# A decode-attention kernel on one core: each tile of keys and values loaded in two transfers of 64 lanes, from two issuing engines

## The chip, the cores and the metric

The kernel runs on one core of one Trainium2 chip. Its engines are TensorE (PE), VectorE (DVE), ScalarE (ACT), GpSimd (POOL) and SyncE (SP); transfers between memory and the on-chip lanes are carried by the core's 16 DMA engines, on behalf of a queue that belongs to the engine that issued them. The metric is the device time of one execution in microseconds (us); lower is better.

## The reference, cut to what matters

Two branches share one layer-normed input and are summed with it. Branch A is attention with a cache: 4 sequences, one new token each, 32 heads of 128, 4096 cached positions. Branch B is a small gated MLP.

```python
q = (xn @ wq).reshape(4, 1, 32, 128).transpose(0, 2, 1, 3)
scores = einsum('bhqd,bhkd->bhqk', q, k_cache) * 128 ** -0.5
p = softmax(scores)
o = einsum('bhqk,bhkd->bhqd', p, v_cache)
A = o.transpose(...).reshape(4, 1, 4096) @ wo
B = gated_mlp(xn)                  # w_in 640 x 1728, w_out 864 x 640
return x + A + B
```

All inputs are bf16. k_cache and v_cache are 134.2 MB each; wq and wo are 5.2 MB each, w_in 2.2 MB, w_out 1.1 MB. Every byte is read once.

## The kernel before, in words

The work on the cache is cut into NT = 32 steps: a step i is one sequence b and one group hg of four heads (HT = 4, HG = 8 groups). Its keys are one tile of 128 lanes x 16384 bf16: the 4 x 4096 rows of 128 are laid over the lanes in order, so that a lane holds 128 consecutive rows (NC = 128), 32 KB in one piece in memory, and a tile has 4096 KB. Its values are a tile of the same form. Lanes 0 to 31 belong to the first head of the group, and so on.

Keys, values and the first weights live in a ring of five slots (pool `kv`, KV_SLOTS = 5; `slot`). `load(which, i)` (L118) takes a slot and issues the transfer; in the kernel before every such transfer is one instruction on SP (L123), except that of the last tile of values, which is cut along its rows into four (V_CUTS). `pump` (L140) issues loads in the fixed list `loads` (K0, K1, V0, K2, V1, K3, ...) as far as its bookkeeping `used` says that the occupant of the slot has been read. It is called once before the loop, once after the MLP, and at the end of every step.

A step (the loop at the end of the function) has the following parts. `product` (L457, DVE) multiplies a half of the key tile in place by the query; `fold_half` (L466, DVE) adds its two halves; `sums` (L475, PE) adds up the rest with the identity into PSUM; `row_sums` (L486, DVE) gives scores. For the maximum: `lane_max` (L495, DVE), `lay_max` (L501, ACT), `spread_max` (L508, PE), `head_max` (L515, DVE). `exps` (L524 ACT, L533 POOL) forms the exponentials and spreads them over the heads' columns into `pm`. `blocks` (L548, PE) multiplies `pm` with the value tile into `pv_acc`, ACT copies that to `pv_sb` every second step (L558), `gather` (L569, PE) collects. The steps overlap: step i runs the maximum and the exponentials of step i-1 and the value product of step i-1 (of i-2 or earlier near the end, after the positions EXTRA_K in the load list).

The order on PE, DVE, ACT and SP is the order in which the program is written (manual_schedule), so each of these queues is strictly in order: an instruction that waits holds everything behind it on its engine. At the end of step i, `pump` issues the values V(i+1), into the slot of V(i-1) once `blocks(i-1)` has read it, and then the keys K(i+3), into the slot of K(i) once `sums(i, 1)` has read it. Every fourth step `load_wo` (L153) puts 640 KB of wo behind them on SP.

Each DMA instruction signals its landing on one of eight semaphores, handed out in turn over all DMA instructions of the program. An instruction that takes a semaphore waits until the eighth DMA instruction before it has landed.

Of the kernel before, what the change touches and what calls it, by code (L numbers as in the profile page):

```python
# [21 lines left out]
def kernel(  # L22
# [14 lines left out]
    nc = tc.nc  # L37
    P = nc.NUM_PARTITIONS
    Bsz, Sq, D = A_x.shape
    _, H, S, Dh = A_k_cache.shape  # L40
# [39 lines left out]
    def slot(name):  # L80
        return kv.tile([P, SLOT], BF16, tag="kv", name=name)
# [8 lines left out]
    for c0, c1 in ((0, HT), (HT, DC)):  # L90
        t = slot("wq")[:, 0 : (c1 - c0) * HD].rearrange("p (c n) -> p c n", n=HD)
# [13 lines left out]
        out=w_out_sb[:, 0:NFF, :], in_=B_w_out[0 : NFF * P].rearrange("(p k) n -> p k n", k=NFF)  # L105
# [3 lines left out]
    def kv_view(cache, i):  # L109
        hg, b = divmod(i, Bsz)  # L110
        return cache[b, HT * hg : HT * (hg + 1)].rearrange("h s d -> (h s) d").rearrange(
            "(p c) d -> p (c d)", c=NC
        )
# [4 lines left out]
    def load(which, i):  # L118
        cache, tiles = (A_k_cache, k_tiles) if which == "k" else (A_v_cache, v_tiles)
        t = slot("k_nat" if which == "k" else "v_nat")  # L120
        cuts = V_CUTS if (which, i) == ("v", NT - 1) else (0, NC)
        for c0, c1 in zip(cuts, cuts[1:]):
            nc.sync.dma_start(  # L123
                out=t[:, c0 * Dh : c1 * Dh], in_=kv_view(cache, i)[:, c0 * Dh : c1 * Dh]
            )
        tiles[i] = t[:].rearrange("p (c d) -> p c d", d=Dh)

    loads = [("k", 0), ("k", 1)]
# [11 lines left out]
    def pump():  # L140
        while n_loaded[0] < len(loads):
            at = n_loaded[0] + 3 - KV_SLOTS
            if at >= 0 and occupants[at] not in used:
                return
            load(*loads[n_loaded[0]])
            n_loaded[0] += 1
# [6 lines left out]
    def load_wo(j):  # L153
# [23 lines left out]
        out=lane_diag[:],  # L177
        in_=ident_f[:].rearrange("p (h l) -> p l h", h=HT),
# [14 lines left out]
    for e in range(2):  # L193
        nc.vector.tensor_reduce(
            out=sel[:, :, :, e],
            in_=ident_f[:].rearrange("p (g e k h) -> p e k h g", g=CG, e=2, k=GC)[:, e],
# [6 lines left out]
    for hh in range(HT):  # L203
# [3 lines left out]
        out=spread[:],  # L207
        in_=ident[:].rearrange("p (m r) -> p r m", r=HT)[:, :, None, :].to_broadcast(
            [P, HT, HT, LN]
        ),  # L210
# [5 lines left out]
        out=q_lanes[:].rearrange("r b (h l) -> r b h l", h=HT),  # L216
        in_=ident[: HT * Bsz, : HT * Bsz]
# [7 lines left out]
    for hh in range(HT):  # L225
        nc.gpsimd.tensor_copy(
            out=place[:, hh, hh * Bsz : (hh + 1) * Bsz], in_=lane_diag[:, 0:Bsz]
# [18 lines left out]
    for i in range(NSTAT):  # L246
# [5 lines left out]
        out=rstd[:], in_=mv[:, 1:2], func=ACT.Sqrt, bias=eps_tile[:Bsz], scale=1.0  # L252
# [4 lines left out]
        out=xn_bf[:],  # L257
# [9 lines left out]
    for c in range(DC):  # L267
        nc.tensor.transpose(
            out=xnT_ps[:, c, :], in_=xn_v[:, c, :], identity=ident[:Bsz, :Bsz]
# [11 lines left out]
    for c in range(DC):  # L281
        t, i = wq_parts[c]
        for hg in range(HG):
            g = hg % CG
            nc.tensor.matmul(  # L285
                out=q_ps[hg // CG][g * LN : (g + 1) * LN, :],
# [13 lines left out]
    def out_sum(half):  # L300
        return out_ps[OG * half : OG * half + Bsz, :]

    for half in range(2):
        nc.tensor.matmul(
            out=out_sum(half),
# [465 lines left out]
```

## Time and profile before

| what | value |
|---|---|
| time, median of 3 runs | 663.49 us (663.44 to 663.57) |
| the profiled execution's own time | 663.4 us |
| its span, first to last instruction | 661.6 us |
| DVE busy | 491.5 us (74%) |
| PE busy | 348.7 us (53%) |
| POOL busy | 151.3 us (23%) |
| ACT busy | 49.3 us (7%) |
| read from memory | 282.24 MB, 427 GB/s over the span |
| granted TensorE clock, mean | 0.726 |

The span is what the trace covers; the 1.8 us between it and the time of the same execution lie before the first and after the last instruction. A row in the list of groups gives the busy time of a kind of instruction and the idle time of its engine just before it, with what ended that idle time. The DMA rows give the mean busy share of the 16 DMA engines in tenths, and the bytes that they moved; a packet is recorded with its bytes when it ends.

### The profile page before, as it was taken

Reading aid. Unit: us, or ns where it says so; the run is one execution under the profiler, and the core shown is the slowest. Engines: PE = TensorE matmul, PEld = TensorE weight load, DVE = VectorE, ACT = ScalarE, POOL = GpSimd, SP = SyncE. Lnnn points to the kernel's source line nnn. Section 1 sums busy time; section 2 is a strip of 40 time slices with the busy share of each in tenths; the row PEclk is TensorE's granted clock in tenths of the full one; section 3 lists DMA queues with packets and bytes.
Section 4 is the critical chain, followed back from the end, with each engine's and each line's share of the span. In section 5 each row is a group of like instructions: output and inputs, shape, how many; then the busy total and the mean of one; then the engine's idle time right before and its main releaser. Section 6 shows DMA issues by size and latency. Waiting matters only on the chain.

```text
span 661.6 us, 5115 instructions
## 1 busy us (share of the span) xinstructions
PE 348.7 (53%) x2109; PEld 144.6 (22%) x2109; DVE 491.5 (74%) x334; ACT 49.3 (7%) x138; POOL 151.3 (23%) x57
## 2 busy tenths in 40 slices
PE   2526653646445455663745654465643756435567
PEld 1402211212121121221212222121211312112124
DVE  2299797867789677788776698776787899777950
ACT  0201100001000010001000000000100000000010
POOL 3002222112222112222112222112222133122230
PEclk9999676776767777766678657777576577688585
DMA  9999999999999999999999999999999999999997
GB/s 368 432 438 429 430 440 427 440 423 434 442 416 447 424 433 442 423 440 424 433 440 423 440 428 431 442 421 442 422 435 442 422 441 428 427 442 428 429 428 289
DMA packets 11971, 282.57 MB, mean 427 GB/s; under 512 B 1344, under 2 KB 1964, under 8 KB 3244
## 3 DMA queue, kind: packets, MB, share of 16 engines
q1 hardware_dynamic: 11928, 282.25, 99.2%
q8 instruction: 16, 0.26, 0.1%
q14 instruction: 7, 0.06, 0.0%
q10 hardware_dynamic: 20, 0.01, 0.0%
HBM read 282.24 MB, written 0.01 MB: 427 GB/s over the span
## 4 chain that ended last, share of the span: by engine, by line
issue 49%; DMA 25%; POOL 15%; DVE 7%; PE 3%; SPq 1%; ACT 0%; POOLq 0%; DVEq 0%; ACTq 0%
DMA k_nat<-in_A_k_cache_dram 20%; POOL pm L533 15%; DMA wo<-in_A_wo_dram 4%; DVE k_nat L457 4%; DVE k_nat L466 2%; PE s_ps L475 2%; PE pv_acc L548 1%; SPq L123 0%; DVE s_sb L486 0%; PE out_ps L647 0%; PE pv L569 0%; POOL own_sum L593 0%; DVE m L495 0%; SPq L92 0%; SPq L104 0%
## 5 line engine op out<-in xcount | busy, mean ns | idle before, releaser
L457 DVE TENSOR_TENSOR k_nat<-k_nat,qbc 128x8192 bf16<-128x8192 bf16 x64 | 282.8, 4419 | 97.8 <-DMA k_nat<-in_A_k_cache_dram 97.8
L533 POOL TENSOR_TENSOR pm<-p,hmask_bf 128x512 bf16<-128x512 bf16 x32 | 142.5, 4452 | 490.9 <-ACT p L524 490.9
L475 PE MATMUL s_ps<-k_nat,ident 128*128 128x512 bf16 x512 | 189.2, 536 | 68.2 <-DVE k_nat L466 68.2
L466 DVE TENSOR_TENSOR k_nat<-k_nat 128x4096 bf16<-128x4096 bf16 x64 | 151.8, 2372 | 0.0
L548 PE MATMUL pv_acc<-v_nat,pm 128*32 128x512 bf16 x1008 | 88.6, 514 | 39.1 <-POOL pm L533 35.5
L508 PE MATMUL max_ps<-lay,head_scale 128*128 128x32 f32 x64 | 18.7, 383 | 171.4 <-ACT lay L501 171.4
L475 PEld LDWEIGHTS <-ident 128*128 128x128 bf16 x512 | 67.9, 135 | 171.1 <-issue 153.8
L508 PEld LDWEIGHTS max_ps<-lay,head_scale 128*128 128x128 f32 x64 | 14.6, 284 | 186.0 <-ACT lay L501 186.0
L548 PEld LDWEIGHTS <-pm 128*32 128x32 bf16 x1008 | 30.2, 120 | 96.2 <-POOL pm L533 52.0
L486 DVE TENSOR_REDUCE s_sb<-s_ps 128x64 f32<-128x512 f32 x64 | 43.3, 677 | 4.2 <-PE s_ps L475 4.2
L501 ACT ACTIVATE lay<-lane_diag,m 128x32 f32<-128x32 f32 x32 | 10.3, 321 | 395.9 <-DVE m L495 395.9
L602 DVE RECIPROCAL rden<-den 128x16 f32<-128x16 f32 x8 | 2.1, 257 | 32.2 <-PE den L600 32.2
L569 PE MATMUL pv<-sel,pv_sb 128*128 128x8 f32 x128 | 19.4, 279 | 9.3 <-ACT pv_sb L558 9.3
L569 PEld LDWEIGHTS pv<-sel,pv_sb 128*128 128x128 f32 x128 | 17.9, 217 | 17.2 <-ACT pv_sb L558 17.2
L524 ACT ACTIVATE p<-s_sb,nb 128x128 bf16<-128x128 f32 x32 | 12.9, 402 | 63.5 <-DVE nb L515 63.5
L558 ACT COPY pv_sb<-pv_acc 128x512 f32<-128x512 f32 x16 | 9.4, 585 | 91.8 <-PE pv_acc L548 91.8
L495 DVE TENSOR_REDUCE m<-s_sb 128x1 f32<-128x128 f32 x32 | 9.1, 286 | 1.1
L285 PE MATMUL q_ps<-wq,xnT 128*32 128x512 bf16 x40 | 4.5, 631 | 8.3 <-DMA wq<-in_A_wq_dram 8.3
L647 PE MATMUL out_ps<-wo,o_r 128*4 128x320 bf16 x56 | 8.0, 433 | 0.3 <-DMA wo<-in_A_wo_dram 0.3
L292 DVE CAST q_sb<-q_ps 128x512 bf16<-128x512 f32 x1 | 0.7, 691 | 9.3 <-PE q_ps L285 9.3
L515 DVE TENSOR_REDUCE nb<-max_ps 128x1 f32<-128x32 f32 x32 | 5.9, 183 | 0.9 <-PE max_ps L508 0.9
L607 DVE TENSOR_TENSOR o_n<-pv,rden 128x16 bf16<-128x16 f32 x8 | 1.3, 168 | 6.7 <-PE pv L581 6.7
(94 smaller groups left out, 91.4 us busy)
## 6 DMA issues: line engine op xcount, KB each, us to landing
k_nat<-in_A_k_cache_dram SPq DMA_DIRECT2D x32, 4096.0 KB, 37.9
v_nat<-in_A_v_cache_dram SPq DMA_DIRECT2D x31, 4096.0 KB, 33.6
wo<-in_A_wo_dram SPq DMA_DIRECT2D x7, 640.0 KB, 38.1
wq<-in_A_wq_dram SPq DMA_DIRECT2D x1, 4096.0 KB, 12.8
w_sb<-in_B_w_in_dram SPq DMA_DIRECT2D x1, 2160.0 KB, 19.5
v_nat<-in_A_v_cache_dram SPq DMA_DIRECT2D x1, 2048.0 KB, 24.5
wq<-in_A_wq_dram SPq DMA_DIRECT2D x1, 1024.0 KB, 14.8
v_nat<-in_A_v_cache_dram SPq DMA_DIRECT2D x1, 1024.0 KB
```

Source lines behind the costliest of these rows:

```text
L457: nc.vector.tensor_tensor(out=t, in0=t, in1=qbcs[i // Bsz][:, i % Bsz, None, :].to_broadcast([P, HC, Dh]), op=ALU.mult,)
L466: nc.vector.tensor_tensor(out=t[:, :, 0:HD2], in0=t[:, :, 0:HD2], in1=t[:, :, HD2:Dh], op=ALU.add)
L475: nc.tensor.matmul(out=s[:], lhsT=ident[:], rhs=t[:, :, g * RW : (g + 1) * RW], start=(g == 0), stop=(g == n - 1),)
L486: nc.vector.tensor_reduce(out=scores[i][:, half * HC : (half + 1) * HC], in_=sums_ps.pop((i, half))[:], axis=AX.X, op=ALU.add,)
L495: nc.vector.tensor_reduce(out=m1[:], in_=scores[i][:], axis=AX.X, op=ALU.max)
L501: nc.scalar.activation(out=d[:], in_=lane_diag[:], func=ACT.Copy, scale=maxes[i][:, 0:1])
L508: nc.tensor.matmul(out=ps[:], lhsT=head_scale[:], rhs=maxes[i][:], start=True, stop=True)
L524: nc.scalar.activation(out=p[:], in_=scores.pop(i)[:], func=ACT.Exp, bias=nb[:], scale=scale_qk, accum_out=acc[hg % NACC][:, b : b + 1],)
L533: nc.gpsimd.tensor_tensor(out=p_m[b][:, :, e : e + GC * HT].rearrange("p g (c h) -> p g c h", h=HT), in0=p[:].rearrange("p (g c) -> p g c" ...
L548: nc.tensor.matmul(out=pv_acc[g * LN : (g + 1) * LN, :], lhsT=pm[:, c // GC, :], rhs=v_nat[:, c : c + GC, :].rearrange("p c d -> p (c d)") ...
L558: nc.scalar.copy(out=pv_sb[:], in_=pv_acc[:])
L569: nc.tensor.matmul(out=pvs[hg][:, :, b - 1 : b + 1], lhsT=pv_sb[:, k * Dh : (k + 1) * Dh], rhs=sel[:, k, :, :], start=(k == 0), stop=stop ...
```

## The change

In `load`, each tile of keys and values is loaded by two instructions instead of one: lanes 0 to 63 by one issued from SP, lanes 64 to 127 by one issued from ACT. Both move the same rows of 32 KB as before. The last tile of values keeps its four transfers over all 128 lanes on SP, and the weights stay as they were. So 63 tiles are split: 63 DMA instructions more, and 63 on ACT's queue where there were 4.

```diff
         cuts = V_CUTS if (which, i) == ("v", NT - 1) else (0, NC)
+        lanes = ((0, P // 2, nc.sync), (P // 2, P, nc.scalar))
+        if len(cuts) > 2:
+            lanes = ((0, P, nc.sync),)
         for c0, c1 in zip(cuts, cuts[1:]):
-            nc.sync.dma_start(
-                out=t[:, c0 * Dh : c1 * Dh], in_=kv_view(cache, i)[:, c0 * Dh : c1 * Dh]
-            )
+            for p0, p1, eng in lanes:
+                eng.dma_start(
+                    out=t[p0:p1, c0 * Dh : c1 * Dh],
+                    in_=kv_view(cache, i)[p0:p1, c0 * Dh : c1 * Dh],
+                )
```

In the instruction order of the changed program the two DMA instructions of `pump` stand on ACT after the copy `pv_sb` (L558 before, L563 now) and ahead of `lay_max` of the same step. The first one on ACT, for lanes 64 to 127 of K0, stands right after the square root of the layer norm.

## Prediction

> **What bounds the kernel now.** I read the page's slices first, then its queues and chain, then waits and the order of time around one step.
>
> ```profile
> DMA  9999999999999999999999999999999999999997
> GB/s 368 432 438 429 430 440 427 440 423 434 442 416 447 424 433 442 423 440 424 433 440 423 440 428 431 442 421 442 422 435 442 422 441 428 427 442 428 429 428 289
> q1 hardware_dynamic: 11928, 282.25, 99.2%
> ...
> k_nat<-in_A_k_cache_dram SPq DMA_DIRECT2D x32, 4096.0 KB, 37.9
> v_nat<-in_A_v_cache_dram SPq DMA_DIRECT2D x31, 4096.0 KB, 33.6
> ```
>
> The 16 DMA engines are busy from end to end, nearly all of it for SP's queue (q1). The last column of the two issue rows is the time from issue to landing.
>
> ```profile
> 260.17 4.42 DVE L457 TENSOR_TENSOR k_nat<-k_nat,qbc 128x8192 bf16<-128x8192 bf16 x1 [4.38 <-DMA k_nat<-in_A_k_cache_dram]
> ...
> 275.06 0.33 SPq L123 DMA_DIRECT2D v_nat<-in_A_v_cache_dram  x1
> ...
> 279.47 4.42 DVE L457 TENSOR_TENSOR k_nat<-k_nat,qbc 128x8192 bf16<-128x8192 bf16 x1 [1.02 <-DMA k_nat<-in_A_k_cache_dram]
> ...
> 282.00 0.33 SPq L123 DMA_DIRECT2D k_nat<-in_A_k_cache_dram  x1
> ...
> 284.90 0.32 ACT L501 ACTIVATE lay<-lane_diag,m 128x32 f32<-128x32 f32 x1 [9.20 <-DVE m L495]
> ```
>
> This is one step in order of time. Both products start when their keys land, 19.30 us apart; two tiles (8.389 MB) arrive in it, so 434.6 GB/s, or 9.65 us a tile. The 33.6 to 37.9 us to landing are 3.5 to 3.9 tiles: SP issues that far ahead. The wait list agrees:
>
> ```profile
> DVE k_nat L457 <- DMA k_nat<-in_A_k_cache_dram: 97.8, 25, 5.6
> ```
>
> DVE, the busiest engine after the DMAs, waits 97.8 us for keys in 25 steps (3.9 us each). So the rate of the transfers is the bound. A last view, at 0.2 us a slice from 404 to 412 us, shows how the rate comes about:
>
> ```profile
> GB/s 492 1147 328 328 164 164 328 1147 492 328 164 164 328 1147 492 328 164 164 328 983 655 328 164 164 328 819 819 328 164 164 328 492 1147 328 164 164 328 492 1147 328
> DMA packets 126, 3.60 MB, mean 451 GB/s; under 512 B 16, under 2 KB 16, under 8 KB 16
> ```
>
> 164 GB/s in 0.2 us is one row of 32 KB ending. The pattern returns every six slices with 16 rows in it (328 + 1147 + 492 + 328 + 164 + 164): each engine moves one row in about 1.2 us, one after another, and the engines keep their places over the window: ten of the 16 end within 0.4 us.
>
> **The change part by part.**
>
> *Issuing.* SP's 63 instructions keep their 0.33 us each; ACT gains 63 of 0.33 us (its only earlier ones took 0.23 to 0.56): 21 to 35 us on an engine that is busy 49.3 us. Cover: ACT's instructions for keys wait, as SP's did at 282.00, for the PE sums; `lay_max` behind them started at 284.90, because its own input came only then. Two issues take 0.66 us of these 2.9: cost 0. If ACT came later than that, `spread_max`, `head_max`, the second product and `exps` would follow, on DVE's 3.9 us of waiting for keys. ACT's wait for values (275.06) needs `blocks(i-1)`, whose `exps` stands ahead of it on ACT.
>
> *The eight semaphores.* Two instructions a tile: only four tiles may be under way. A tile's half waits for the half four tiles back: for V(i+1) that is V(i-1), which it overwrites anyway; for K(i+3) it is K(i+1), landed at 279.47, before the 282.00 at which the slot is free. After each wo the turn shifts by one, and SP's half of K(i+3) waits for V(i), about 289 (279.47 + 9.65): 7 us late, on a queue that had 24 us of transfers left when the V came at 275.06 (33.6 - 9.65). Behind it on SP stand loads alone. Cost 0.
>
> *Completions.* The 1344 packets under 512 B are 84 instructions x 16 engines; 63 more instructions add 1008. The window above contains such a tile's end (16 of them) and its pattern keeps its six slices, so one costs under a slice: between 0 and 63 x 0.2 = 12.6 us; a gain is not excluded, as the other queue's rows could fill a gap at a tile's end. I take 0, since the 16 leave no trace.
>
> *Start and tail.* K0's SP half now waits for wq to land (13.6 us), ACT's is issued at about 4 us and takes turns with wq: wq and the query move by up to 2.1 MB / 434.6 = 4.8 us. Ahead of the queue lie 4.3 MB of weights, then K0 and K1, 8.4 MB: it does not run dry. Behind the last split tile all is as before. 0 for both.
>
> *The transfers themselves.* This decides, and the trace does not show it: no large transfer into 64 lanes exists. If what limits to 434.6 GB/s is the 16 engines, two queues sharing them lose nothing: 0 us. If it is the side of the lanes, 64 lanes take half, 217 GB/s, and the halves reach the full rate only if at every moment half of the engines write low lanes and half high ones. Each engine serves the queues in turn, row by row. Two engines that start on the low lanes together each go at half speed, finish together, and meet again on the high ones. Engines a share x of a row apart lose less: a pair of rows takes 2 - x times as long. The window says that engines go nearly together and keep their distance. Ends: 0 and 63 x 9.65 = 608 us. With ten of 16 ends within 0.4 us I take a distance of 0.3 us, a quarter of a row: factor 1.75, +0.75 x 608 = 456 us. I take this end and not 0 because the nearest row I have, the window, shows the engines in step.
>
> [...]
>
> *Sum.* 0 + 0 + 0 + 0 + 456 on a span of 661.6: 1117.6, with the 1.8 us around it 1119 us. The profiled execution took 663.4, the median is 663.49: the same.
>
> **The rivals.**
>
> 1. *The halves interleave cleanly (not slower).* The limit is the engines, or pairs fall into opposite turns, as they would if one engine had precedence at the lanes: 663.5 us. For it: all 16 engines still carry every byte, and nothing is added to the chain. Faster is hard: the idle 0.8% (5.3 us) is less than the about 1.5 us before the first row ends plus the 5 us after the last (656.6 to 661.6). Only a higher rate would do it, as if 434.6 became the best slice's 447: 608 x 2.8% = 17 us, 646.
> 2. *Full serialisation.* Pairs go exactly in step, so every tile takes 19.3 us: 663.4 + 608 = 1271. For it: a tile lands when its last engine is done, so the worst pair counts; against it: the window's ends are spread over 1.2 us.
> 3. *The queues get out of step.* Pairs alternate well, but each wo (128 rows of 5 KB, 8 per engine) takes turns with eight 32 KB rows of ACT's queue, so that SP's halves fall eight rows behind; when ACT's queue is empty, SP's rows go alone, at half rate if lanes limit: 8 x 1.2 = 9.6 us for each of the six wo loads within the loop, 58 us: 721. If lanes don't limit, this costs nothing.
> 4. *ACT's queue becomes the bound.* Were ACT held 7 us in every step, the 2.2 us of cover and DVE's 3.9 would leave 0.9 us x 32 = 29: 692. Against it: the order puts the late wait on SP.
>
> **How the numbers follow.** No change means within 0.2% (1.3 us), about what this kernel's measurement can tell. Forecast, lanes limit with pairs partly in step (factor 1.4 to 1.9, 906 to 1211): 0.36. Rival 2 (1211 to 1275): 0.17. Rivals 3, 4 and lesser losses (665 to 905): 0.22. Rival 1: 0.25, of it 0.18 within 0.2% and 0.07 faster. Slower: 0.36 + 0.17 + 0.22 = 0.75. The range 662 to 1272 leaves out the faster cases and little above; the likeliest case's own range is 906 to 1211.
>
> **What would show it.** Two queues with about equal megabytes; a rate of 220 to 310 GB/s in the slices with the DMA share still at 9; a row's time in 0.2 us slices of 1.6 to 2.4 us instead of 1.2; DVE's wait for keys several times 97.8 us; `lay_max` still waiting for DVE, not for an issue. I am wrong if the slices show 420 to 440 again (rival 1), if only stretches behind the wo loads are slow (3), or if DVE's wait for keys shrinks and its wait for `max_ps` grows (4).

## The result and the profile after

The changed kernel takes 1209.74 us (1201.9 to 1216.4, four runs) against 663.53 us before: a ratio of 1.8227 with a 95% interval of 1.8125 to 1.8329. The forecast of 1119 us was of the right kind and 91 us short. The profiled execution took 1206.46 us, its span is 1204.4 us.

The page of the changed kernel, slices, queues and issues (the last column is again the time from issue to landing):

```profile
DMA  9999999999999999999999999999999999999996
GB/s 251 272 223 215 226 224 226 222 233 240 250 271 242 234 249 246 242 226 238 236 234 229 217 233 235 245 229 227 237 231 226 220 228 241 241 244 246 244 227 184
q1 hardware_dynamic: 7896, 150.13, 52.8%
q10 hardware_dynamic: 5060, 132.13, 46.6%
...
k_nat<-in_A_k_cache_dram ACTq DMA_DIRECT2D x32, 2048.0 KB, 39.0
k_nat<-in_A_k_cache_dram SPq DMA_DIRECT2D x32, 2048.0 KB, 70.8
...
wq<-in_A_wq_dram SPq DMA_DIRECT2D x1, 4096.0 KB, 28.1
```

The DMA engines are still busy from end to end, now for two queues with nearly equal bytes (q1 is SP's, q10 ACT's), and in all slices but the last they move 215 to 272 GB/s, where they moved 416 to 447 in all but the first and the last. A row of 32 KB holds its engine for longer: ACT's queue has only the 63 x 64 = 4032 rows of the upper halves, so 46.6% of 16 engines' 1204.4 us makes 2.23 us a row, against about 1.2 us before. No row escapes it: from 100 to 1100 us the trace has 7035 rows of 32 KB, and none of them took under 1.6 us. The bytes are the same and the compute engines do the same work (DVE 492.3 us busy, before 491.5), so the time that was added is in the transfers.

From the list of waits of the changed kernel (total, times, longest):

```profile
DVE k_nat L462 <- DMA k_nat<-in_A_k_cache_dram: 503.4, 30, 25.9
...
ACT lay L506 <- DVE m L500: 746.4, 29, 38.1
...
ACT lay L506 <- DMA wo<-in_A_wo_dram: 56.8, 2, 35.3
```

DVE waits for keys for 503.4 us, before 97.8. `lay_max` on ACT still waits for its own input, except in two steps: there a DMA instruction ahead of it on ACT waited for a semaphore last used by a wo load, 56.8 us in all.

The rows of the two queues can be told apart in short windows. A packet stands in these views at its start, and not at its end as the section on the profile before has it: in the trace of the kernel before, a row recorded at 276.157 us with a duration of 1.213 us is over at 277.370 us, and a completion and a row of wo are recorded at 277.371 and 277.377 us, where it leaves its engine free. The patterns read so far hold for starts as they would for ends. Two windows of 1.2 us of the changed kernel, 103.6 to 104.8 us and 106.0 to 107.2 us:

```profile
DMA packets 13, 0.43 MB, mean 355 GB/s; under 512 B 0, under 2 KB 0, under 8 KB 0
...
q1 hardware_dynamic: 13, 0.43, 154.0%
```

```profile
DMA packets 13, 0.43 MB, mean 355 GB/s; under 512 B 0, under 2 KB 0, under 8 KB 0
...
q10 hardware_dynamic: 13, 0.43, 151.4%
```

In the first, 13 rows start and all are SP's; 2.4 us later 13 rows start and all are ACT's. At this time most of the 16 engines do go from low to high lanes together, one turn in about 2.4 us. The share above 100% counts the whole time of rows that start in the window. Later in the run the picture is not so clean, and that turned out to matter.

### The profile page after: what moved, and what is told of

Its sections match the earlier page's. It is cut to its first block, busy times and chain, and to the rows that moved or that the text cites. A ratio compares the mean times of both kernels' runs of the same rounds, so it can differ in the third digit from the quotient of the medians.

```text
span 1204.4 us, 5378 instructions
## 1 busy us (share of the span) xinstructions
PE 388.6 (32%) x2109; PEld 162.8 (14%) x2109; DVE 492.3 (41%) x334; ACT 49.4 (4%) x138; POOL 151.3 (13%) x57
## 2 busy tenths in 40 slices
DMA packets 12980, 282.59 MB, mean 235 GB/s; under 512 B 2352, under 2 KB 2972, under 8 KB 4252
## 3 DMA queue, kind: packets, MB, share of 16 engines
q10 hardware_dynamic: 5060, 132.13, 46.6%
## 4 chain that ended last, share of the span: by engine, by line
another core or an unknown queue 49%; DVE 32%; DMA 7%; PE 6%; issue 5%; SPq 0%; ACT 0%; ACTq 0%; DVEq 0%
DVE k_nat L462 17%; DVE k_nat L471 10%; PE s_ps L480 3%; DMA k_nat<-in_A_k_cache_dram 3%; DVE s_sb L491 3%; DMA wq<-in_A_wq_dram 2%; PE pv_acc L553 2%; DMA wo<-in_A_wo_dram 2%; DVE m L500 1%; PE out_ps L652 0%; PE den L605 0%; DVE nb L520 0%; DVE o_r L640 0%; DVE rden L607 0%
## 5 line engine op out<-in xcount | busy, mean ns | idle before, releaser
L462 DVE TENSOR_TENSOR k_nat<-k_nat,qbc 128x8192 bf16<-128x8192 bf16 x64 | 282.9, 4421 | 541.9 <-DMA k_nat<-in_A_k_cache_dram 503.4
L480 PE MATMUL s_ps<-k_nat,ident 128*128 128x512 bf16 x512 | 199.9, 561 | 62.3 <-DVE k_nat L471 62.3
L553 PE MATMUL pv_acc<-v_nat,pm 128*32 128x512 bf16 x1008 | 111.7, 621 | 209.3 <-DMA v_nat<-in_A_v_cache_dram 209.3
L480 PEld LDWEIGHTS <-ident 128*128 128x128 bf16 x512 | 70.6, 142 | 174.8 <-issue 160.8
L553 PEld LDWEIGHTS <-pm 128*32 128x32 bf16 x1008 | 40.4, 138 | 274.2 <-issue 249.6
L506 ACT ACTIVATE lay<-lane_diag,m 128x32 f32<-128x32 f32 x32 | 10.3, 321 | 824.4 <-DVE m L500 746.4
L607 DVE RECIPROCAL rden<-den 128x16 f32<-128x16 f32 x8 | 2.1, 258 | 70.8 <-PE den L605 70.8
L574 PE MATMUL pv<-sel,pv_sb 128*128 128x8 f32 x128 | 23.5, 311 | 8.5 <-ACT pv_sb L563 8.5
L574 PEld LDWEIGHTS pv<-sel,pv_sb 128*128 128x128 f32 x128 | 22.0, 259 | 16.7 <-ACT pv_sb L563 16.7
L563 ACT COPY pv_sb<-pv_acc 128x512 f32<-128x512 f32 x16 | 9.4, 586 | 184.8 <-PE pv_acc L553 184.8
## 6 DMA issues: line engine op xcount, KB each, us to landing
k_nat<-in_A_k_cache_dram SPq DMA_DIRECT2D x32, 2048.0 KB, 70.8
wq<-in_A_wq_dram SPq DMA_DIRECT2D x1, 4096.0 KB, 28.1
```

The costliest lines, as they stand in the source:

```text
L462: nc.vector.tensor_tensor(out=t, in0=t, in1=qbcs[i // Bsz][:, i % Bsz, None, :].to_broadcast([P, HC, Dh]), op=ALU.mult,)
L480: nc.tensor.matmul(out=s[:], lhsT=ident[:], rhs=t[:, :, g * RW : (g + 1) * RW], start=(g == 0), stop=(g == n - 1),)
L506: nc.scalar.activation(out=d[:], in_=lane_diag[:], func=ACT.Copy, scale=maxes[i][:, 0:1])
L553: nc.tensor.matmul(out=pv_acc[g * LN : (g + 1) * LN, :], lhsT=pm[:, c // GC, :], rhs=v_nat[:, c : c + GC, :].rearrange("p c d -> p (c d)") ...
L563: nc.scalar.copy(out=pv_sb[:], in_=pv_acc[:])
L574: nc.tensor.matmul(out=pvs[hg][:, :, b - 1 : b + 1], lhsT=pv_sb[:, k * Dh : (k + 1) * Dh], rhs=sel[:, k, :, :], start=(k == 0), stop=stop ...
```

## The experiments

**Is it the two queues or the 64 lanes?** Theory A (lanes): a transfer of lanes 0 to 63, or of 64 to 127, runs at about half rate whoever issues it. Theory B (queues): two queues taking turns on the DMA engines, or ACT held by the issues, cost the time. Two kernels part them. The first issues both halves from SP:

```diff
-        lanes = ((0, P // 2, nc.sync), (P // 2, P, nc.scalar))
+        lanes = ((0, P // 2, nc.sync), (P // 2, P, nc.sync))
```

> The lanes 0 to 63 and 64 to 127 stay two transfers, but both are issued from SP, so no second queue takes part and ACT issues none of them. If 64 lanes of one side carry only half the rate (lanes theory): each half of a tile takes about as long as a whole tile did, 63 x 9.65 us more, 1200 to 1275 us, and the rows take about 2.4 us each. If the two queues are at fault (their turns on the DMA engines, or the issues that hold ACT), the time falls back to 663 to 680 us.

It took 1315.47 us, a ratio of 1.9816 (1.9768 to 1.9864), with 208 to 218 GB/s in all slices but the first and the last:

```profile
GB/s 336 213 213 214 213 215 213 213 210 213 211 213 212 210 209 211 218 209 208 211 210 211 211 210 213 208 211 208 211 209 211 212 210 215 210 210 211 216 214 244
```

One queue is slower than two, so the second queue isn't the cause. The second kernel keeps both queues and cuts each tile by columns:

```diff
-        for c0, c1 in zip(cuts, cuts[1:]):
-            nc.sync.dma_start(
+        halves = len(cuts) == 2
+        if halves:
+            cuts = (0, HC, NC)
+        for c0, c1 in zip(cuts, cuts[1:]):
+            eng = nc.scalar if halves and c0 else nc.sync
+            eng.dma_start(
                 out=t[:, c0 * Dh : c1 * Dh], in_=kv_view(cache, i)[:, c0 * Dh : c1 * Dh]
             )
```

> Each tile is again two transfers, one from SP and one from ACT, with the same number of instructions, the same waits on the eight semaphores and the same issues on ACT, but each covers all 128 lanes and half of the columns (rows of 16 KB). Lanes theory: 663 to 670 us, rate near 430 GB/s. Two-queue theory: as slow as the changed kernel, 1150 to 1250 us.

It took 667.27 us, a ratio of 1.0049 (1.0032 to 1.0066). Theory B falls. Two queues, 126 instructions, ACT's issues and the tighter semaphores together cost 3.6 us here, and part of that may be the rows of 16 KB (21044 packets instead of 11971).

**Which 64 lanes?** Even lanes from SP, odd lanes from ACT, otherwise as changed:

```diff
-        lanes = ((0, P // 2, nc.sync), (P // 2, P, nc.scalar))
+        lanes = ((0, P, nc.sync), (1, P, nc.scalar))
...
-                    out=t[p0:p1, c0 * Dh : c1 * Dh],
-                    in_=kv_view(cache, i)[p0:p1, c0 * Dh : c1 * Dh],
+                    out=t[p0:p1:st, c0 * Dh : c1 * Dh],
+                    in_=kv_view(cache, i)[p0:p1:st, c0 * Dh : c1 * Dh],
```

Here st is 2 for the split tiles.

> As the changed kernel, two transfers of 64 lanes from SP and from ACT, but of the even and the odd lanes, so that each half is spread over the whole range of lanes. If only the range that a transfer covers counts: 663 to 690 us. [...] If the number of lanes in a transfer counts: about 1210 us.

It took 664.62 us, a ratio of 1.0015 (1.0004 to 1.0025), at 416 to 442 GB/s in all slices but the first and the last:

```profile
GB/s 378 421 442 416 436 441 422 439 431 426 441 433 428 437 420 439 437 425 441 424 433 437 424 437 430 430 427 440 433 434 429 436 426 435 434 425 435 440 419 269
...
k_nat<-in_A_k_cache_dram ACTq DMA_DIRECT2D x32, 2048.0 KB, 23.1
k_nat<-in_A_k_cache_dram SPq DMA_DIRECT2D x32, 2048.0 KB, 35.8
...
wq<-in_A_wq_dram SPq DMA_DIRECT2D x1, 4096.0 KB, 17.8
```

So 64 lanes in a transfer are no handicap (664.62 us); 64 lanes of one side are (1209.74 us). This kernel has the same count of instructions, completions, issues on ACT and semaphores as the changed one, so it also prices all of these together: 0.9 us.

**Lanes, or the place in memory?** A half tile of neighbouring lanes is also one piece of 2 MB in memory. This kernel keeps lanes 0 to 63 and 64 to 127 but reads alternate rows:

```diff
-            for p0, p1, eng in lanes:
+            for n, (p0, p1, eng) in enumerate(lanes):
+                rows = slice(n, P, len(lanes))
                 eng.dma_start(
                     out=t[p0:p1, c0 * Dh : c1 * Dh],
-                    in_=kv_view(cache, i)[p0:p1, c0 * Dh : c1 * Dh],
+                    in_=kv_view(cache, i)[rows, c0 * Dh : c1 * Dh],
                 )
```

> As the changed kernel (lanes 0 to 63 from SP, 64 to 127 from ACT), but the two transfers read every second row of the tile in memory, SP's the even and ACT's the odd ones. The rows land in other lanes than they should, so the heads are mixed and the numbers computed are others; the work is the same. If the side of the lanes sets the rate, nothing gets better: about 1210 us. If it is the place in memory (a half tile is one piece of 2 MB there, the even rows are spread over 4 MB), the time falls back to 663 to 670 us.

It took 1222.19 us, a ratio of 1.8412 (1.8375 to 1.8449). Reading alternate rows did not bring the time back. SP and ACT read the same rows here as in the kernel with even and odd lanes, and only the lanes that they write differ (1222.19 against 664.62 us). So the limit is on the side of the lanes.

**Neighbouring lanes of both sides.** Three transfers a tile, all on SP, the middle one with 64 neighbouring lanes:

```diff
-        lanes = ((0, P // 2, nc.sync), (P // 2, P, nc.scalar))
+        lanes = ((P // 4, 3 * P // 4, nc.sync), (0, P // 4, nc.sync), (3 * P // 4, P, nc.sync))
```

> All on SP, three transfers a tile: lanes 32 to 95 in one, then 0 to 31, then 96 to 127. [...] If lanes do not matter, 663 to 690 us.

The two runs took 1237.83 and 1271.47 us. With the middle half of a tile at 434.6 GB/s and the two quarters at half of it, an estimate is 4.8 + 9.65 = 14.5 us a tile, 965 us in all; with every part at half, 1271. Taken alone that speaks against lanes 32 to 95 being any better. But the test mixes three kinds of transfer, and two theories are open: any 64 neighbouring lanes are slow, or only 64 of one side. So I measured one kind at a time: the kernel before, and behind each whole tile one small transfer of 64 lanes into a spare tile, on SP. The three kernels differ in `extra` only:

```diff
         tiles[i] = t[:].rearrange("p (c d) -> p c d", d=Dh)
+        if len(cuts) == 2:
+            extra = slice(P // 4, 3 * P // 4)    # or slice(0, P // 2), or slice(0, P, 2)
+            x = spare.tile([P, XW], BF16, tag="spare", name="spare")
+            nc.sync.dma_start(out=x[extra], in_=kv_view(cache, i)[extra, 0:XW])
```

> The kernel before, and behind each of its 63 whole tiles one more transfer on SP, of lanes 32 to 95 and 2560 bytes a lane (164 KB) into a spare tile that nothing reads. At the full rate of 434.6 GB/s it is 0.38 us a tile, 24 us in all (687 us); at half rate 0.75 us, 47 us (711 us). [...] If any 64 neighbouring lanes have half the rate: as slow as lanes 0 to 63 in the sister kernel. The three are read against each other, since rows of 2560 bytes have a cost of their own.

> The same with lanes 0 to 63: half rate by both theories, 47 us more than before (711 us), and about 24 us more than with the even lanes.

> The same with the 64 even lanes, which the even and odd split showed to run at the full rate: 24 us more than before (687 us), and the least of the three.

| extra transfer of 64 lanes | time | over before (663.65) | per tile |
|---|---|---|---|
| even lanes | 688.98 us | 25.3 us | 0.40 us |
| lanes 32 to 95 | 689.23 us | 25.6 us | 0.41 us |
| lanes 0 to 63 | 778.52 us | 114.9 us | 1.82 us |

The middle lanes are as fast as the even ones (0.41 and 0.40 us a tile), and near the full rate: the same bytes at 434.6 GB/s make 0.38 us. The lower 64 lanes cost 4.5 times as much as the even ones for the same bytes, and more than twice the 47 us that half rate would make. The slices of this kernel show where that goes:

```profile
GB/s 379 416 395 398 410 404 390 403 390 385 391 395 389 381 387 392 375 381 385 372 375 386 367 383 384 375 386 389 389 383 387 384 384 379 386 381 376 375 320 81
DMA packets 17012, 292.91 MB, mean 377 GB/s; under 512 B 2352, under 2 KB 2972, under 8 KB 8284
```

The extra bytes are 10.3 of 292.9 MB, and the whole stream falls from 427 to 377 GB/s. The one-sided transfer slows what goes beside it, not only itself: in this kernel's trace the 8192 rows of 32 KB, nearly all of them of whole tiles, took 1.351 us each on average, in the kernel before 1.216 us. Over 16 engines that is 69 of the 114.9 us.

**Does a whole tile suffer beside half tiles?** Only the values split, the keys whole on SP:

```diff
-        if len(cuts) > 2:
+        if len(cuts) > 2 or which == "k":
             lanes = ((0, P, nc.sync),)
```

> Only the 31 whole tiles of values are split into lanes 0 to 63 (SP) and 64 to 127 (ACT); the keys come in one transfer of 128 lanes on SP. If each split tile costs the same wherever it stands (the changed kernel's 546 us over 63 tiles, 8.7 us each): 31 x 8.7 = 269 us more, 933 us. If the loss comes from the whole run being in one pattern of low and high halves, which the whole rows of the keys break up: well below, 700 to 850 us.

Both cases are far off: the two runs took 1261.45 and 1308.41 us, more than with all tiles split. The profile is of the longer one. Its window from 400 to 450 us:

```profile
DMA packets 360, 9.90 MB, mean 198 GB/s; under 512 B 58, under 2 KB 58, under 8 KB 58
...
q1 hardware_dynamic: 278, 7.80, 79.9%
q10 hardware_dynamic: 82, 2.10, 21.1%
```

Half of a step's bytes, the keys, come in whole transfers here, and still the total is 198 GB/s. Had the keys kept 434.6 GB/s and the values run at half of it, a step would take 9.65 + 19.3 = 29 us; the steps whose first products start at 442.83 and 481.58 us are 38.8 us apart. The keys' transfers, unchanged in form, have lost their rate as well: 4096 of the 6208 rows of 32 KB on SP's queue are theirs, and only 843 of the 6208 took under 2 us, so that at least 3253 rows of keys took 2 us or more.

**Is it the step between engines?** My forecast had engines meet at the same side because of the turns between the queues. Then a tiny transfer that uses only some of the engines should give these one turn and undo it. Ahead of two tiles of values (or, in the last kernel, of eleven):

```diff
+        if (which, i) in (("v", 10), ("v", 21)):
+            some = slice(0, 32, 4)    # 8 lanes; the control has slice(0, 64, 4), 16 lanes
+            x = const.tile([P, 256], BF16, name=f"nudge{i}")
+            nc.sync.dma_start(out=x[some], in_=kv_view(cache, i)[some, 0:256])
```

> The changed kernel, and ahead of SP's half of V10 and of V21 one tiny transfer more on SP: 8 lanes (0, 4, ... 28) of 512 bytes into a spare tile that nothing reads. [...] If engines that share lanes are kept in step by strict turns between the two queues, the tiny row uses up one turn of half of the engines in almost no time, so these then write high lanes while their partners write low ones: from V10 on the rate should jump from about 235 to above 400 GB/s, and fall back from V21 on; about 11 of 32 steps at 9.65 us a tile instead of 18.3 make 1020 us. If steps play no part (the loss is in the 64 lanes of a transfer as such): no change in rate, 1200 to 1220 us.

> [...] By both theories as the changed kernel: 1200 to 1220 us, 235 GB/s throughout.

The 8 lanes took 1223.04 us, the 16 lanes 1209.44 us. The page of the 8-lane kernel counts 32 packets more than that of the changed kernel for its two transfers, 8 rows and 8 completions each, where the 63 half tiles more in the changed kernel brought 16 completions each (2352 packets under 512 B instead of 1344); so only half of the engines took part, as intended. The rate did not move: no slice of the 8-lane kernel is above 265 GB/s. In the last kernel the tiny transfers have other numbers of lanes:

```diff
+    NUDGES = {("v", 4 + m): 2 * m + 1 for m in range(8)}
+    NUDGES.update({("v", 18 + m): 4 * m + 4 for m in range(3)})
```

> As the run with 8 lanes, but with other sets of engines. [...] If no separation of engines helps, the loss is not one of step between two engines: 1200 to 1230 us and 220 to 250 GB/s throughout.

It took 1216.24 us, with 217 to 254 GB/s in every slice from the third on. No rate rose, but the trace shows that a tiny transfer doesn't do what the expectations have it do. In the 8-lane kernel each of the first one's eight rows (461 to 469 us) is followed by a row of ACT's queue on the same engine, that one by the tiny transfer's own completion of 4 bytes, and this by another row of ACT's (the start of each meets the end of the one ahead to 0.02 us). The completion takes a turn as the row does. So each engine gave two turns of SP's queue and not one, and after them it wrote low and high lanes in the same order against the other engines as before. The eight rows between the tiny row and its completion, the only ones out of that order, took 2.28 to 2.46 us, no less than the others. That is a hint against the step idea for these engines, but the three kernels don't test it as they were meant to.

Two windows of 1.2 us in the 8-lane kernel, from 507.2 and from 509.6 us, show engines out of step:

```profile
DMA packets 11, 0.33 MB, mean 273 GB/s; under 512 B 1, under 2 KB 1, under 8 KB 1
...
q10 hardware_dynamic: 6, 0.20, 63.4%
q1 hardware_dynamic: 5, 0.13, 41.9%
```

```profile
DMA packets 11, 0.36 MB, mean 300 GB/s; under 512 B 0, under 2 KB 0, under 8 KB 0
...
q1 hardware_dynamic: 6, 0.20, 62.1%
q10 hardware_dynamic: 5, 0.16, 51.8%
```

Here rows of both queues start side by side, unlike at 104 us in the changed kernel. A window shorter than a row doesn't give the rate; over 100 us from 520 to 620 this kernel moves 234 GB/s, and from 380 to 460, before its first tiny transfer, 230.

The changed kernel's own trace says how much the mixture is worth. I counted for each moment from 50 to 1150 us how many rows of 32 KB of each queue are under way (SP's write the low lanes, ACT's the high ones) and added up their rates. With one to three on the side that has fewer (28% of the time) they make 219 GB/s, with seven or more on both sides (22%) 246. The same count with even and odd lanes gives 433 for seven or more of each queue. So engines spread over both sides gain about an eighth and not the full rate. The records don't name a row's engine, so whether certain engines stay in step with each other while others move apart can't be read from them.

## Why the prediction was right, and where it was not

**What bounds the kernel** stood as read: the transfers. With their rate nearly halved every other engine only waits longer.

**Issuing, semaphores, completions, tail at 0** was right to within 0.9 us, by the even and odd split, which has all of them. One detail was wrong: I wrote that the order puts the late wait for a semaphore on SP, where only loads stand behind it. In two steps it fell on ACT (the 56.8 us above). What it cost there is not measured by itself; DVE's 503.4 us of waiting for keys can hide it. With even and odd lanes such a wait came once, 12.0 us, and is within the 0.9 us.

**The start** was mis-sized: I moved wq by up to 4.8 us, and it landed 28.1 us after its issue instead of 12.8. With even and odd lanes it landed after 17.8 us, so taking turns with ACT's queue cost the forecast's 5 us, and the other 10 us come with the one-sided halves. What this delay added to the time is not measured by itself.

**The transfers themselves.** The choice of the slow end was right. The two ends, 0 and 608 us, are near what the runs give, 0.9 us with even and odd lanes and 652 us (1315.47 - 663.68) with both halves on one queue. The term was 0.75 x 608 = 456 us; measured it is 1209.74 - 663.53 = 546 us, a factor of 1.90 on the split tiles instead of 1.75. That puts the time just inside the likeliest case's own range (906 to 1211); the four runs, 1201.9 to 1216.4 us, lie on both sides of its edge.

Of the reason given for the factor one part is borne out: "Each engine serves the queues in turn, row by row", and at 104 us most engines went from side to side together (13 rows of SP's, and 2.4 us later 13 of ACT's). The other part, a distance x of a quarter of a row and 2 - x from it, was my assumption and is not shown by any run. The engines did move apart later, but with both sides in use the rate was 246 GB/s instead of 219, and no row from 100 to 1100 us took under 1.6 us, where by that assumption engines on opposite sides should need the 1.2 of the kernel before. Whether the assumption holds for some of the engines the tiny transfers, at two turns each, don't decide. So the 1.75 was near by luck, and why two queues with opposite halves don't fill both sides is not settled.

What the runs do show is that a one-sided transfer holds up other transfers: 114.9 us for 10.3 MB, whole key tiles slowed beside split value tiles (at least 3253 of their 4096 rows at 2 us or more), and probably the three-part tiles at 1238 to 1271 us where 965 was worked out from each part alone. How one transfer comes to hold up another is not shown by any run.

**The rivals.** Clean interleaving (663.5) is refuted for halves of one side; its time is what even and odd lanes give. Full serialisation (1271) is what one queue gives, and a little more: 1315.47, as the steady rate there is about 211 GB/s and not half of 434.6. Two queues regain about 106 us of that. So this rival was closer to the result (1.82, of the 1.98 of one queue) than its chance of 0.17 had it. The queues out of step (721) did occur, as SP's halves land 70.8 us after their issue and ACT's 39.0; but all slices are slow, not only those behind a wo load, and a shift of the same kind with even and odd lanes (35.8 and 23.1 us) costs next to nothing, so it isn't what made the time. ACT as the bound did not occur.

## What to carry to other kernels

Where transfers bound a kernel, ask first which lanes each transfer writes at a time: here 64 lanes of one side halved the rate (about 211 GB/s with both halves on one queue), 64 lanes spread over both sides didn't (416 to 442 GB/s with even and odd lanes). If a tile has to be cut, cut its columns (0.5% here) or take every second lane (0.15%), and don't expect a second queue to add rate to engines that are already 99% busy (664.62 us with two queues and even and odd lanes, 663.68 us before). A small one-sided transfer in a saturated stream cost 4.5 times what the same bytes cost over both sides (1.82 against 0.40 us a tile), so price it by what it holds up. And before an experiment rests on the turns of a queue, count a transfer's completions among them (here each took a turn, as its row did).

## What the runs showed of the hardware that was not expected

- A transfer of 164 KB into lanes 0 to 63 behind each whole tile cost 1.82 us, the same into lanes 32 to 95 or the even lanes 0.41 and 0.40 us.
- Splitting only the values (1261 and 1308 us) was slower than splitting keys and values (1209.74 us), though the keys then came in whole transfers.
- Two transfers of alternate lanes on two queues, each with 64 lanes, ran at the rate of one transfer of 128 (664.62 against 663.68 us).
- The 4-byte completion of a tiny transfer took a turn of its queue on each engine, as a row of 32 KB does: behind it, as behind the tiny row, a row of the other queue came first (the 8-lane kernel, 461 to 469 us).
